# Spectral row groups between the w1 products, and another order inside the norm's backward

## The chip, the cores and the metric

The kernel runs on one core of a Trainium2 chip. The metric is the device time of one execution in microseconds (us). Engines are named as in the profile: PE is TensorE (matmul) and PEld its weight load, DVE is VectorE, ACT is ScalarE, POOL is GpSimd, SP is SyncE. Each engine works through its own queue in order; engines wait for one another through semaphores.

## The reference

The reference is the forward pass of a two-part layer and its gradients. Shapes: x is 2048 x 448 (sequence S by width D), w1 is 2048 x 1792, w2 is 1792 x 2048, the spectral weights are 2048 x 225 (real and imaginary). Inputs and outputs are bf16.

```python
def _A_ref(x, w_r, w_i):
    X = rfft2(x)                       # over sequence and width
    return irfft2(X * (w_r + 1j * w_i))
def _B_ref(x, w1, b1, w2, b2):
    h = _layernorm(x)
    u = gelu(einsum("bsd,sf->bdf", h, w1) + b1)
    return (einsum("bdf,fs->bds", u, w2) + b2).transpose(0, 2, 1)
h  = x + _A_ref(_layernorm(x), w_r, w_i)
h2 = h + _B_ref(_layernorm(h), w1, b1, w2, b2)
```

Outputs are h2 and the gradients of x, w_r, w_i, w1, b1, w2 and b2 for a given grad_out. The change lies in the backward pass: the gradient dh behind the second norm, the spectral transform of dh, and the gradient of x behind the first norm.

## The kernel before

Everything is tiled over 128 partitions. A row index h = 0..15 (NT = 16) stands for the 16 interleaved sets of 128 sequence positions. The two-dimensional transform is done with matmuls against tables, in steps: fft_rows folds four sets h of a group g (three VectorE operations, L303 to L305, into the tile eo) and makes 16 matmuls of 128 x 128 x 128 (L311), four per PSUM tile; each PSUM tile is then copied to zt, on ScalarE ("a", L194) or VectorE ("v", L196) as the string "aava" says. fft_cols then makes the columns, cmul multiplies by the weights, ifft_cols and ifft_rows come back.

The forward pass fills the first 186 us. Behind it lies what the change touches:

1. The w1 loop (L624 to L633). For each h, 14 matmuls (L632) accumulate the product of w1T and du in one PSUM tile pd of 449 columns; column 448 holds the sum that the mean needs. The w1T tiles are loaded by transposing DMAs on SP's queue, through a ring of four.
2. norm_back, called once for each h, turns pd into the row set dh[:, h, :]. It makes the sum of products nm2 (L601, VectorE, with a read-out of the accumulator), the mean's column nm1 (L606, VectorE), the scaled copy v of the whole tile (L608, ScalarE), and two VectorE operations (L611, L612) that put these together. v uses nm1; L611 uses nm2 and v.
3. Behind the loop, fft_rows on dh for groups 0, 1 and 2, then the first block of the w2 gradient, gw2(0) (L653: 16 matmuls and four copies on ScalarE), then fft_rows for group 3, whose matmuls are put behind gw2(0) by hand.
4. fft_cols, cmul, ifft_cols and 16 times ifft_rows. Each ifft_rows ends in a PSUM tile py, on which norm_back is called with mean=False: L601, then v (L610, ScalarE, without a bias), L611, L612, and a store of the gradient of x on POOL's queue.
5. gw2(1) to gw2(13), each 16 matmuls and four copies, three on ScalarE and one on VectorE ("aaav"). In the program they follow the spectral step, but they fill TensorE's time between its matmuls.
6. The w1 gradient (L723, 256 matmuls, all copies on ScalarE), with a second cmul on VectorE for the gradients of w_r and w_i (grad_w) put in after its fourth row set.

The order of the instructions on each engine is not that of the program text alone. A planner at build time walks all instructions by priority, which is their place in the program, and gives an engine that it believes free the first instruction that it believes ready; on the chip the queues then keep that order. `with tc.issue_after(x)` puts what is inside behind x on x's engine. Tiles come from rings: PSUM has three buffers for matmul results (ps_mm: pd and the gradients' blocks) and five for the spectral step (ps_sp); in SBUF, eo comes from a ring of three, v from one of three, junk and the outputs from one of ten. The planner adds the waits for data, for buffers and for PSUM tiles.

Of the kernel before, what the change touches and what calls it, by code (L numbers as in the profile page):

```python
# [13 lines left out]
ALU = mybir.AluOpType  # L14
# [3 lines left out]
P = 128  # L18
S = 2048
D = 448  # L20
DF = 225
F = 1792
NFB = 14
NT = 16
NR = 16
# [88 lines left out]
def kernel(  # L114
# [21 lines left out]
    ve, ac, po, pe = nc.vector, nc.scalar, nc.gpsimd, nc.tensor  # L136
# [7 lines left out]
    def slot(i, shape, name):  # L144
        return big.tile(shape, BF16, tag=f"s{i}", name=name)

    def w4(shape, name):
        return ring.tile(shape, BF16, tag="w4", bufs=4, name=name)

    def e4(shape, name):  # L150
        return ring.tile(shape, BF16, tag="e4", bufs=3, name=name)

    def k1(shape, name, dtype=BF16):
        return ring.tile(shape, dtype, tag="k1", bufs=10, name=name)

    def f2(shape, name):
        return ring.tile(shape, F32, tag="f2", bufs=3, name=name)

    def col(n, name, dtype=F32):
        return ring.tile([P, n], dtype, tag=name, bufs=4, name=name)  # L160

    def ps_mm(shape, dtype=F32):
        return psum.tile(shape, dtype, tag="mm", bufs=3, name="ps_mm")

    def ps_sp(shape, dtype=F32):
        return psum.tile(shape, dtype, tag="sp", bufs=5, name="ps_sp")

    def ld(out, in_, eng=None):
        return (eng or nc.sync).dma_start(out=out, in_=in_)
# [4 lines left out]
    def ld_t(out, in_):  # L174
        return nc.sync.dma_start(out=out, in_=in_, transpose=True)
# [11 lines left out]
    def ld_t4(out, in_):  # L187

        ld_t(out[:, 0:3, :], in_[:, 0:384])
        ld_t(out[:, 3, :], in_[:, 320:448])  # L190

    def ev(out, in_, on):
        if on == "a":
            ac.copy(out=out, in_=in_)  # L194
        else:
            ve.tensor_copy(out=out, in_=in_)  # L196
# [33 lines left out]
    def load_w(dst, on):  # L230
        on(ld, dst[:, 0, :], A_w_r.rearrange("(q r) k -> q (r k)", r=NR))
        on(ld, dst[:, 1, :], A_w_i.rearrange("(q r) k -> q (r k)", r=NR))
# [67 lines left out]
    def fft_rows(src, zt, g, on, behind=None):  # L300
        eo = e4([P, 4, D], "eo")
        a, b = src[:, 4 * g:4 * g + 4, 1:224], src[:, 4 * g:4 * g + 4, 447:224:-1]
        ve.tensor_tensor(out=eo[:, :, 1:224], in0=a, in1=b, op=ALU.add)  # L303
        ve.tensor_tensor(out=eo[:, :, 225:448], in0=a, in1=b, op=ALU.subtract)
        fold = ve.tensor_copy(out=eo[:, :, 0:225:224], in_=src[:, 4 * g:4 * g + 4, 0:225:224])  # L305
        for i in range(4):
            h = 4 * g + i
            pz = ps_sp([P, 4, P])
            with tc.issue_after(behind.ins) if behind is not None else nullcontext():
                for c, o in enumerate((0, 97, 225, 320)):  # L310
                    last = pe.matmul(pz[:, c, :], lhsT=eo[:, i, o:o + P], rhs=kf[:], start=True, stop=True)  # L311
            ev(zt[:, :, :, 8 * h:8 * h + 8], pz[:, :, :].rearrange("p c (s k) -> p c s k", k=8), on[i])
        return last, fold
# [114 lines left out]
    du = slot(7, [P, NFB, 450], "du")  # L428
# [147 lines left out]
    for t0 in range(0, NT, 4):  # L576
# [3 lines left out]
        for j in range(NFB):  # L580
            for i in range(4):
                pe.matmul(p2[i][:], lhsT=w2c[t0 // 4][:, j, i * P:(i + 1) * P], rhs=gT[:, j, :],  # L582
                          start=(j == 0), stop=(j == NFB - 1))
        for i in range(4):
# [3 lines left out]
                                    op0=ALU.add, op1=ALU.add)  # L588
# [3 lines left out]
    for h in range(NT):  # L592
        junk = ring.tile([P, D], BF16, tag="gj", bufs=1, name="junk")
# [2 lines left out]
    ac.copy(out=gb2b[:], in_=gb2[:])  # L596

    def norm_back(ps, mean, xhat, rstd_c, rneg_c, base, out):
        nm2 = col(1, "nm2")
        junk = k1([P, D], "junk")  # L600
        ve.tensor_tensor_reduce(out=junk[:], in0=ps[:, 0:D], in1=xhat, scale=rneg_c, scalar=0.0,  # L601
                                op0=ALU.mult, op1=ALU.add, accum_out=nm2[:])
        v = f2([P, D], "v")
        if mean:
            nm1 = col(1, "nm1")
            ve.tensor_scalar(out=nm1[:], in0=ps[:, D:D + 1], scalar1=rstd_c, scalar2=-1.0 / D,  # L606
                             op0=ALU.mult, op1=ALU.mult)
            ac.activation(out=v[:], in_=ps[:, 0:D], func=ACT.Identity, scale=rstd_c, bias=nm1[:])  # L608
        else:
            ac.activation(out=v[:], in_=ps[:, 0:D], func=ACT.Copy, scale=rstd_c)  # L610
        ve.scalar_tensor_tensor(out=junk[:], in0=xhat, scalar=nm2[:], in1=v[:], op0=ALU.mult, op1=ALU.add)  # L611
        ve.tensor_tensor(out=out, in0=junk[:], in1=base, op=ALU.add)  # L612

    dh = go_r
    w1Tv = B_w1.rearrange("(q h) f -> h q f", h=NT)
    df0 = consts.tile([P, 6 * DF], BF16, tag="df", name="df0")
    di1 = consts.tile([P, 4 * DF], BF16, tag="di", name="di1")
    w_b = slot(6, [P, 2, XW], "w_b")
    for h in range(NT):
        if h == 4:  # L620
            goT = slot(4, [P, 4, S], "goT")
            with tc.issue_after(w1T_last.ins):
                ld_t4(goT[:], grad_out[0])
        if h == 4:  # L624
            with tc.issue_after(w1T_last.ins):
                ld(df0[:], hnd["df0"].ap())
                ld(di1[:], hnd["di1"].ap())
        w1T = w4([P, NFB, P], "w1T")
        w1T_last = ld_t(w1T[:], w1Tv[h])
        pd = ps_mm([P, D + 1])  # L630
        for j in range(NFB):
            pe.matmul(pd[:], lhsT=w1T[:, j, :], rhs=du[:, j, 0:D + 1], start=(j == 0), stop=(j == NFB - 1))  # L632
        norm_back(pd, True, hln[:, h, :], rstd_h[:, h:h + 1], rneg_h[:, h:h + 1], go_r[:, h, :], dh[:, h, :])  # L633


    with tc.issue_after(w1T_last.ins):
        load_w(w_b, lambda load, out, in_: load(out, in_))
    zt2 = slot(2, [P, 4, NR, P], "zt2")
    for g in range(3):
        fft_rows(dh, zt2, g, "aava")  # L640

    g_t = slot(0, [P, 4, F], "g_t")
    ld_t4(g_t[:], gT_d[:])
# [22 lines left out]
    for h in range(NT):  # L666
        if h % 4 == 0:
            xr = e4([P, 4, D], "xr")
            ld(xr[:], xln_d[:, h:h + 4, :], po)
        py = ifft_rows(ab2, di1, h)  # L670
        gx = k1([P, D], "gx")
        norm_back(py, False, xr[:, h % 4, :], rstd_x[:, h:h + 1], rneg_x[:, h:h + 1], dh[:, h, :], gx[:])
        st(rows(out_1[0])[:, h, :], gx[:])
# [43 lines left out]
    for h in range(NT):  # L717
        s4 = w4([P, F], "s4")
        for n in range(4):
            wdt = 512 if n < 3 else 256  # L720
            pw = ps_mm([P, 512])
            for c in range(4):
                pe.matmul(pw[:, 0:wdt], lhsT=hlnT[:, c, h * P:(h + 1) * P],  # L723
                          rhs=du_t[:, c, 512 * n:512 * n + wdt], start=(c == 0), stop=(c == 3))
# [37 lines left out]
```

## Time and profile before

| | |
|---|---|
| median of 3 runs | 382.5 us (381.94 to 383.04) |
| the profiled execution's own time | 377.61 us |
| its span, first to last instruction | 375.8 us |
| granted TensorE clock | 0.999 of full speed |
| PE busy | 350.0 us, 93% of the span |
| DVE, ACT, POOL busy | 235.5, 215.5, 61.3 us |
| w1 products (L632) | 224 matmuls, 186.2 to 229.3 us |
| span from 229.3 to 240.5 us | PE busy 9.02 of 11.20 us |
| span from 283.0 to 317.2 us | PE busy 33.76 of 34.20 us |
| span from 317.2 to 342.0 us | PE busy 23.66 of 24.80 us |

How to read it: the time behind a line is one profiled execution, on the profile's own clock that starts with the first instruction. A row of a timeline has start, duration, engine, line, operation, output, inputs, shapes and count, and in square brackets how long the engine stood idle before it and what ended that. In the lists of waits a row says who waited for whom, the sum, the number of times and the longest. Matmuls are pipelined and their ends are modelled, so that a short hole in TensorE's queue shows smaller as idle time than in the starts of the rows: work it out from the starts.

### The profile page before, as it was taken

The page shows a single profiled execution, that of the slowest core. Times are in us where ns is not written, and L with a number is a line of the kernel's source. Part 1 is how long each engine was busy: PE and PEld are TensorE (multiplying, and loading weights), DVE is VectorE, ACT ScalarE, POOL GpSimd, SP SyncE. Part 2 cuts the span into 40 slices and gives each one's busy share as a digit, 9 for nine tenths or more (in the row PEclk, how much of TensorE's full clock was granted, in tenths as well). Part 3 has the DMA queues.
Part 4 walks back from the last instruction along what each step waited for, and adds up shares of the span by engine and source line. Part 5 has one row for each costly group of instructions (what it writes and reads, how often), then busy time and mean ns, then how long its engine had stood idle before and what let it go on. Part 6 is the DMA issues. An engine that isn't in the chain of part 4 may idle for free.

```text
span 375.8 us, 5768 instructions
## 1 busy us (share of the span) xinstructions
PE 350.0 (93%) x2115; PEld 200.8 (53%) x2115; DVE 235.5 (63%) x557; ACT 215.5 (57%) x415; POOL 61.3 (16%) x107
## 2 busy tenths in 40 slices
PE   0798999989999999999999997999989999999996
PEld 0455666666655555555555555556655555554553
DVE  4863679876745999522267777268995666598000
ACT  3685555345659998740022224967655656676664
POOL 1000000001113111421120000101013422256111
PEclk9999999999999999999999999999999999999999
DMA  7999998999999999891998891932864544956533
GB/s 280 261 291 269 290 253 241 298 324 221 301 251 347 357 333 382 330 285 24 219 204 173 172 254 64 256 83 90 184 181 181 196 162 149 356 211 229 200 153 147
DMA packets 132524, 86.48 MB, mean 230 GB/s; under 512 B 91952, under 2 KB 123824, under 8 KB 131984
## 3 DMA queue, kind: packets, MB, share of 16 engines
q1 hardware_dynamic: 124304, 55.78, 59.9%
q0 software_dynamic: 8048, 30.31, 21.4%
q8 instruction: 16, 0.26, 0.3%
q14 instruction: 12, 0.10, 0.1%
q10 hardware_dynamic: 144, 0.03, 0.0%
HBM read 32.81 MB, written 30.76 MB: 169 GB/s over the span
## 4 chain that ended last, share of the span: by engine, by line
PE 70%; DVE 13%; DMA 7%; ACT 7%; issue 1%; SPq 1%; ACTq 0%; DVEq 0%
PE ps_mm L632 11%; PE ps_mm L653 9%; PE ps_mm L723 8%; PE ps_sp L582 7%; PE ps_mm L434 7%; PE ps_mm L515 6%; PE ps_sp L515 5%; PE ps_mm L582 4%; DMA w2T<-in_B_w_dram 3%; DMA xs_b<-xs_d 2%; DVE t_r L362 2%; DVE t_i L363 2%; DVE gg L349 2%; PE ps_sp L321 2%; PE ps_sp L311 1%; ACT xln L296 1%
## 5 line engine op out<-in xcount | busy, mean ns | idle before, releaser
L194 ACT CAST s<-ps_mm 128x512 bf16<-128x512 f32 (+1 forms) x107 | 57.2, 559 | 19.2 <-PE ps_mm L723 7.5
L653 PE MATMUL ps_mm<-goT,g_t 128*128 128x512 bf16 x224 | 55.3, 379 | 1.5 <-ACT s L194 1.3
L434 PE MATMUL ps_mm<-go_nat,w2T 128*128 128x448 bf16 x224 | 51.2, 361 | 2.1 <-DMA w2T<-in_B_w_dram 2.1
L723 PE MATMUL ps_mm<-du_t,hlnT 128*128 128x512 bf16 (+1 forms) x256 | 49.9, 352 | 0.6 <-ACT s L194 0.5
L608 ACT ACTIVATE v<-ps_mm,nm,rstd_h 128x448 f32<-128x448 f32 x16 | 11.6, 723 | 56.9 <-DVE nm L606 54.9
L632 PE MATMUL ps_mm<-du,w1T 128*128 128x449 bf16 x224 | 43.1, 353 | 0.0
L723 PEld LDWEIGHTS <-hlnT 128*128 128x128 bf16 x256 | 25.0, 98 | 23.1 <-issue 0.9
L582 PE MATMUL ps_sp<-gT,w2c 128*128 128x448 bf16 x140 | 35.6, 352 | 0.0
L172 POOL DMA_DIRECT2D out_dram<-s x29 | 15.6, 539 | 119.0 <-ACT s L194 81.9
L632 PEld LDWEIGHTS <-w1T 128*128 128x128 bf16 x224 | 21.8, 97 | 21.1
L582 PEld LDWEIGHTS <-w2c 128*128 128x128 bf16 x224 | 21.9, 98 | 20.5
L515 PEld LDWEIGHTS <-w1c 128*128 128x128 bf16 x224 | 21.8, 98 | 20.5 <-issue 1.8
L653 PEld LDWEIGHTS <-g_t 128*128 128x128 bf16 x224 | 21.7, 97 | 19.9 <-issue 1.3
L434 PEld LDWEIGHTS <-w2T 128*128 128x128 bf16 x224 | 22.0, 100 | 18.0 <-DMA w2T<-in_B_w_dram 3.3
L349 DVE TENSOR_TENSOR gg<-ps_sp,gi 128x450 bf16<-128x450 f32 x28 | 16.2, 620 | 17.1 <-ACT gi L346 17.1
L582 PE MATMUL ps_mm<-gT,w2c 128*128 128x448 bf16 x84 | 25.0, 352 | 0.0
L515 PE MATMUL ps_mm<-hln,w1c 128*128 128x448 bf16 x112 | 24.3, 352 | 0.7 <-DVE b1col L504 0.5
L194 ACT CAST eo<-ps_sp 128x450 bf16<-128x450 f32 x32 | 17.3, 540 | 12.7 <-PE ps_sp L407 12.4
L311 PE MATMUL ps_sp<-kf,eo 128*128 128x128 bf16 x128 | 9.8, 230 | 15.6 <-DVE mv_x L281 12.1
L515 PE MATMUL ps_sp<-hln,w1c 128*128 128x448 bf16 x112 | 23.1, 352 | 0.0
L587 DVE SCALAR_TENSOR_TENSOR h<-ps_sp,b2col,hr 128x448 bf16<-128x448 f32 x10 | 6.3, 679 | 25.1 <-PE ps_sp L582 25.1
L610 ACT ACTIVATE v<-ps_sp,rstd_x 128x448 f32<-128x448 f32 x16 | 10.1, 634 | 15.7 <-DVE nm L601 15.7
(146 smaller groups left out, 625.7 us busy)
## 6 DMA issues: line engine op xcount, KB each, us to landing
w1c<-in_B_w_dram SPq DMA_DIRECT2D x7, 1024.0 KB, 8.2
w2c<-in_B_w_dram SPq DMA_DIRECT2D x8, 896.0 KB, 11.1
out_dram<-s POOLq DMA_DIRECT2D x14, 512.0 KB, 3.1
out_dram<-s POOLq DMA_DIRECT2D x15, 448.0 KB, 2.8
xs_d<-xs SPq DMA_DIRECT2D x1, 1800.0 KB, 7.7
xs_b<-xs_d SPq DMA_DIRECT2D x1, 1800.0 KB, 8.6
x<-in_A_x_dram SPq DMA_DIRECT2D x4, 448.0 KB, 4.4
go_nat<-in_grad_out_dram SPq DMA_DIRECT2D x2, 896.0 KB, 7.1
```

The source lines that it names most:

```text
L172: return (eng or po).dma_start(out=out, in_=in_)
L194: ac.copy(out=out, in_=in_)
L311: last = pe.matmul(pz[:, c, :], lhsT=eo[:, i, o:o + P], rhs=kf[:], start=True, stop=True)
L349: ve.tensor_tensor(out=gg[:], in0=pr[:], in1=gi[:], op=op)
L434: pe.matmul(pg[:], lhsT=w2T[j][:, t, :], rhs=go_nat[:, t, :], start=(t == 0), stop=(t == NT - 1))
L515: pe.matmul(pu[:], lhsT=wc[:, h, o:o + P], rhs=hln[:, h, :], start=(h == 0), stop=(h == NT - 1))
L582: pe.matmul(p2[i][:], lhsT=w2c[t0 // 4][:, j, i * P:(i + 1) * P], rhs=gT[:, j, :], start=(j == 0), stop=(j == NFB - 1))
L608: ac.activation(out=v[:], in_=ps[:, 0:D], func=ACT.Identity, scale=rstd_c, bias=nm1[:])
L610: ac.activation(out=v[:], in_=ps[:, 0:D], func=ACT.Copy, scale=rstd_c)
L632: pe.matmul(pd[:], lhsT=w1T[:, j, :], rhs=du[:, j, 0:D + 1], start=(j == 0), stop=(j == NFB - 1))
L653: mm = pe.matmul(pw[:], lhsT=g_t[:, c, j * P:(j + 1) * P], rhs=goT[:, c, 512 * n:512 * n + 512], start=(c == 0), stop=(c == 3))
L723: pe.matmul(pw[:, 0:wdt], lhsT=hlnT[:, c, h * P:(h + 1) * P], rhs=du_t[:, c, 512 * n:512 * n + wdt], start=(c == 0), stop=(c == 3))
```

## The change

Two edits.

- In the w1 loop, before the products of h = 10 and of h = 14, fft_rows is called for group 0 and group 1. Its matmuls are put behind the last product issued so far (w1_last). The tile zt2 is allocated ahead of the loop. Behind the loop only group 2 is left (group 3 stays where it was).
- In norm_back, the sum of products (nm2) is made after nm1 and v instead of ahead of them. With mean=False there is no nm1, and there the sum comes after v.

```diff
     def norm_back(ps, mean, xhat, rstd_c, rneg_c, base, out):
-        nm2 = col(1, "nm2")
-        junk = k1([P, D], "junk")
-        ve.tensor_tensor_reduce(out=junk[:], in0=ps[:, 0:D], in1=xhat, scale=rneg_c, scalar=0.0,
-                                op0=ALU.mult, op1=ALU.add, accum_out=nm2[:])
+
         v = f2([P, D], "v")
         if mean:
             nm1 = col(1, "nm1")
...
             ac.activation(out=v[:], in_=ps[:, 0:D], func=ACT.Identity, scale=rstd_c, bias=nm1[:])
         else:
             ac.activation(out=v[:], in_=ps[:, 0:D], func=ACT.Copy, scale=rstd_c)
+        nm2 = col(1, "nm2")
+        junk = k1([P, D], "junk")
+        ve.tensor_tensor_reduce(out=junk[:], in0=ps[:, 0:D], in1=xhat, scale=rneg_c, scalar=0.0,
+                                op0=ALU.mult, op1=ALU.add, accum_out=nm2[:])
         ve.scalar_tensor_tensor(out=junk[:], in0=xhat, scalar=nm2[:], in1=v[:], op0=ALU.mult, op1=ALU.add)
...
+    zt2 = slot(2, [P, 4, NR, P], "zt2")
     for h in range(NT):
+
+        if h in (10, 14):
+            fft_rows(dh, zt2, h // 4 - 2, "aava", w1_last)
...
-            pe.matmul(pd[:], lhsT=w1T[:, j, :], rhs=du[:, j, 0:D + 1], start=(j == 0), stop=(j == NFB - 1))
+            w1_last = pe.matmul(pd[:], lhsT=w1T[:, j, :], rhs=du[:, j, 0:D + 1], start=(j == 0), stop=(j == NFB - 1))
...
-    zt2 = slot(2, [P, 4, NR, P], "zt2")
-    for g in range(3):
-        fft_rows(dh, zt2, g, "aava")
+    fft_rows(dh, zt2, 2, "aava")
```

## The prediction

> **What bounds the kernel now.** I read the page first: the engines' shares and the 40 slices.
>
> ```profile
> PE 350.0 (93%) x2115; PEld 200.8 (53%) x2115; DVE 235.5 (63%) x557; ACT 215.5 (57%) x415; POOL 61.3 (16%) x107
> ```
>
> TensorE is the bound, so I looked only for stretches in which its queue stands still because another engine is late. The chain of work that ended last, listed in order of time, names one right behind the w1 loop (columns: start, duration, what):
>
> ```profile
> 186.37 42.93 PE ps_mm L632 x224
> 229.30 0.68 PE ps_sp L311 x12
> 230.00 0.73 ACT v L608
> 230.76 0.69 DVE junk L611
> 231.78 0.68 DVE junk L601
> 232.70 0.72 ACT v L608
> 233.42 1.94 ACT zt L194 x5
> ...
> 236.82 0.50 ACT s L194
> 237.36 1.02 PE ps_mm L653 x4
> 238.38 0.89 PE ps_sp L311 x16
> ```
>
> The loop itself is solid matmul. Behind it 48 short row matmuls (L311) fill the five PSUM buffers, and their copies queue on ScalarE behind the last two norm rows. The TensorE timeline has two holes there, 0.83 and 1.13 us. Next I took VectorE's timeline for one norm row of the loop:
>
> ```profile
> 203.28 0.68 DVE L601 CUSTOM_DVE_ANT_0 junk<-ps_mm,hln,rneg_h 128x448 bf16<-128x448 f32 x1
> 203.88 0.08 DVE L601 DVE_READ_ACCUMULATOR2_ANT nm<- 128x1 f32 x1
> 203.88 0.21 DVE L606 TENSOR_SCALAR nm<-ps_mm,rstd_h 128x1 f32<-128x1 f32 x1
> 204.97 0.68 DVE L611 SCALAR_TENSOR_TENSOR junk<-hln,nm,v 128x448 bf16<-128x448 bf16 x1 [0.87 <-ACT v L608]
> 205.69 0.39 DVE L612 TENSOR_TENSOR go_r<-junk,go_r 128x448 bf16<-128x448 bf16 x1
> 206.00 0.68 DVE L601 CUSTOM_DVE_ANT_0 junk<-ps_mm,hln,rneg_h 128x448 bf16<-128x448 f32 x1
> ```
>
> A row takes 2.72 us from L601 to L601; TensorE's 14 products take 42.93/16 = 2.68. VectorE is therefore the slower one, and each of the folds (L303 to L305) of groups 0 to 2 pushes it back another 0.67 (0.54 outside the gap, and a shifted start). By the last row it is 2.5 us late (231.78 against products that ended near 229.3). Last I took the second use of the same helper, where the spectral step ends (L610): the waits, then ScalarE's and TensorE's timelines for one row.
>
> ```profile
> ACT v L610 <- DVE nm L601: 15.7, 14, 1.9
> ```
> ```profile
> 291.52 0.63 ACT L610 ACTIVATE v<-ps_sp,rstd_x 128x448 f32<-128x448 f32 x1 [1.02 <-DVE nm L601]
> 292.05 1.06 ACT L194 CAST s<-ps_mm 128x512 bf16<-128x512 f32 x2
> 293.00 0.56 ACT L194 CAST eo<-ps_sp 128x450 bf16<-128x450 f32 x1
> ```
> ```profile
> 290.93 2.54 PE L653 MATMUL ps_mm<-goT,g_t 128*128 128x512 bf16 x11
> 293.61 0.26 PE L411 MATMUL ps_sp<-eo,kinv 128*128 128x225 bf16 x1
> ```
>
> There ScalarE stands idle 1.02 us for a reduction it does not need the value of; its in-order queue then delivers eo late, and TensorE, out of fill matmuls at 290.93 + 11 x 0.215 = 293.3, waits 0.3 us for it.
>
> **The change, part by part.**
>
> *Row groups 0 and 1 moved into the loop.* 32 of the 64 L311 matmuls move. Sixteen take 0.85 to 1.06 us in these rows, so 1.7 to 2.1 us goes into the loop and out of the stretch behind it: nothing on TensorE's sum. Loop end moves from 229.1 to about 230.9. Their eight copies go too: six on ScalarE (0.5 us each; it idles about 2.0 us a row) and two on VectorE (0.60 each, which fit the 0.87 gap). Cover: ScalarE's idle time. Without it, six copies x 0.5 = 3.0 us would delay v rows. No DMA is issued by the step; SP's queue (w1T loads, then w_b) and POOL's keep their order, and zt2's slot has been free since the w2 product read it. The folds already run in the loop at the fourth, eighth and twelfth row and should stay there.
>
> *The mean's column first, in the loop.* The reduction (L601) now stands behind v. Do the two run side by side? In the L610 rows v waits for a reduction that gives it no data; both read the same PSUM tile. I take it that the order holds the other way round as well. Then a row is: column to v 0.34 (203.88 to 204.22), v to the next VectorE step 0.75 (204.22 to 204.97), reduction to its consumer 0.60 + 0.08 + 0.04 = 0.72 (the read-out now stands directly ahead of its user; 0.04 is what L611 to L612 adds), L611 0.72, L612 0.31: 2.84 us, 0.12 more than now, x 16 = 1.9 us on VectorE. The Trainium skill, "PSUM — Partial Sum Buffer", section "PSUM bank collisions raise a hardware error", says that two engines may not touch the same bank and quadrant at once, two reads included, so software has to put them one behind the other. This speaks against the edit; the L610 rows agree, with 14 waits of 15.7 us in all. By that rule the loop row is the 2.84 us above; without it the row would be 2.12 us and the last fold would no longer be late.
>
> *What that does behind the loop.* VectorE's last row ends at 189.09 + 16 x 2.84 + 3 x 0.67 = 236.5 instead of 234.8. Before, a zt copy (0.61) came between it and the last fold; with fewer copies there, the fold follows at once: 236.5 + 1.25 + 0.1 = 237.9 for group 3's matmuls, against 238.2. TensorE's own work would let them start at 230.9 + 0.85 (group 2) + 16 x 0.213 (first gw2 block) = 235.2: VectorE is what is late next. ScalarE was busy without a break from 233.3 to 239.0 and is not any more, so the last zt copies come 0.6 us sooner and the column step begins near 239.9, not 240.53. I take **0.6 us gained**. Ends: TensorE sets the start (235.2, copies included), 2.9 gained; or the three second fold pieces (0.72 each) and three zt copies (0.60) fall outside the gaps, 4.0 later, 3.4 lost. I am nearest to the first value because the present folds show 0.24 us of gap left after two pieces, and a copy is shorter than those. A PSUM buffer of pd is now freed by the reduction's end, 1.77 us into a row: row 12's at about 227.6, wanted for row 15 at 228.1. Covered by 0.5 us only; TensorE would stall for the excess, but VectorE sets the end of that stretch anyway.
>
> *v first, in the second use.* ScalarE's v no longer waits for VectorE: it can start 0.78 us sooner (291.52 less 290.74, L601's start); the reduction waits for v instead, and behind it on VectorE stand L611, L612, the fourth s copy of a gw2 block and later the grad_w products. One hand-over between engines fewer per row. What is TensorE's loss there? From 283.17 to 317.21: 116 gw2 matmuls x 0.215 = 24.9, and 9 rows x 0.78 + 0.39 = 7.4 of short ones: 32.3 of 34.0, idle 1.7. From 317.21 to 339.61: 84 x 0.190 = 15.9 (32.63/172 from the last stretch) and 4.3: 20.2 of 22.4, idle 2.2. Together 3.9 us; 0.78 a row is more than the 0.2 to 0.3 a row lost. Ends: all 3.9 gained, or 5.9 lost (0.66, v and its hand-over, x the nine rows with copies on VectorE). I take 70%, **2.7 us**, because the fill matmuls are placed by a plan that will shift with the new order, and the nearest row (291.52) shows the wait plainly.
>
> **Sum:** 0.6 + 2.7 = 3.3 us. The profiled execution took 377.6 us (span 375.8 and 1.8 around it), so it would be 374.3. The median shown is 382.5, 4.9 above it; less 3.3 it is 379.2.
>
> **The rivals.**
> 1. *Both reads side by side* (no wait between v and the reduction in the loop): group 3 starts at 235.2, 2.3 us more than forecast, 376.9. Against: the L610 waits.
> 2. *The plan eats it*: fewer fill matmuls per row, new holes of the same size; 0.6 stays at most, 382. For: TensorE holes of 0.3 us are small beside a 0.5 us copy.
> 3. *VectorE overruns in the loop*: folds and copies outside the gaps, 4.0 us later than forecast, 383.2.
> 4. *Slower: VectorE's queue in the second use.* The reduction starts 0.66 us later, waiting for v; behind it stands the s copy that gw2 needs for one of its three PSUM buffers. If it comes late by all of that, nine rows cost 5.9 us and the 1.2 of the gain up to 317 is gone: 379.2 + 7.1 = 386.3. It decides from (3.3 - 1.2)/9 = 0.23 us a row. For: VectorE needs 0.60 + 0.72 + 0.72 + 0.31 + 0.60, nearly 3 us, of a 3.5 us row, behind that wait. Against: it idles 0.55 to 1.0 us before L601 now, and the gap for v disappears.
>
> **How the numbers follow.** Forecast 0.50 (own range 377.0 to 381.2), rivals 1 to 4: 0.10, 0.06, 0.08, 0.26. The measured runs spread over 0.3%, 1.1 us, so "same" is 381.4 to 383.6. Faster: forecast and rival 1, 0.60. Same: rival 2 and half of 3, 0.10. Slower: rival 4 and the other half, 0.30. The range runs from 376.2, just past rival 1, to 384.8, the middle of rival 4, leaving out under 2 in 10.
>
> **What the changed profile would show.** In the loop: L311 matmuls in two blocks of 16, rows of 2.84 us on VectorE, reductions released by v; if the rows are near 2.1, rival 1. Behind it: 16 instead of 48 L311 matmuls, group 3 near 237.9. In the second use: no wait of v for L601, reductions waiting for v, and ScalarE's idle 15.7 us gone; TensorE's holes under 1.2 us over the stage. The prediction is wrong if s copies on VectorE hold up TensorE (rival 4), or if the holes stay though v no longer waits.

## The result, and the profile after

| | before | changed |
|---|---|---|
| median (runs) | 382.53 us (6) | 375.85 us (6) |
| ratio, 95% interval | | 0.987 (0.983 to 0.992) |
| profiled execution's time; its span | 377.61; 375.8 us | 375.83; 374.1 us |
| first w1 product starts at | 186.21 us | 189.14 us |
| A: from there to the first column matmul (L329) | 54.32 us | 52.23 us |
| B: from there to the first L411 | 42.25 us | 42.23 us |
| C: from there to the end of the span | 93.02 us | 90.50 us |

The change made the kernel faster, by 1.3% and by 4.8 us if the ratio on record is applied to 382.5; the two medians themselves are 6.7 us apart. The two profiled executions differ by only 1.8 us, because the changed one was 2.9 us later at its first w1 product, where the two programs do not differ yet. So I compare stretches that begin at that product. A is 2.1 us shorter and C 2.5, and B is the same: 4.6 together.

TensorE's timeline of the changed kernel, from the loop to the last row group (start, duration, engine, line, operation, shapes, count, and in brackets the idle time before it):

```profile
189.14 26.99 PE L637 MATMUL ps_mm<-du,w1T 128*128 128x449 bf16 x140
215.97 1.05 PE L311 MATMUL ps_sp<-kf,eo 128*128 128x128 bf16 x16
216.86 10.90 PE L637 MATMUL ps_mm<-du,w1T 128*128 128x449 bf16 x56
227.60 1.05 PE L311 MATMUL ps_sp<-kf,eo 128*128 128x128 bf16 x16
228.49 5.53 PE L637 MATMUL ps_mm<-du,w1T 128*128 128x449 bf16 x28
233.86 1.05 PE L311 MATMUL ps_sp<-kf,eo 128*128 128x128 bf16 x16
234.75 2.98 PE L656 MATMUL ps_mm<-goT,g_t 128*128 128x512 bf16 x12
237.89 1.02 PE L656 MATMUL ps_mm<-goT,g_t 128*128 128x512 bf16 x4 [0.17 <-ACT s L194]
239.12 1.07 PE L311 MATMUL ps_sp<-kf,eo 128*128 128x128 bf16 x16 [0.21 <-DVE eo L305]
```

Two blocks of 16 row matmuls lie between the products and cost 0.9 us each. The holes of 0.83 and 1.13 us behind the loop are gone; those left are 0.17 and 0.21 us. In the kernel before they stood ahead of these row matmuls:

```profile
231.25 0.87 PE L311 MATMUL ps_sp<-kf,eo 128*128 128x128 bf16 x8 [0.83 <-ACT zt L194]
233.25 0.38 PE L311 MATMUL ps_sp<-kf,eo 128*128 128x128 bf16 x4 [1.13 <-DVE zt L196]
```

The last group waits for its fold on VectorE (L305), 49.98 us behind the first product (52.01 before). VectorE's timeline around a fold shows what a row costs now ("..." stands for rows left out; the first and the last row shown are the loop's first and last):

```profile
192.02 0.22 DVE L603 TENSOR_SCALAR nm<-ps_mm,rstd_h 128x1 f32<-128x1 f32 x1 [0.79 <-PE ps_mm L637]
...
211.84 0.21 DVE L603 TENSOR_SCALAR nm<-ps_mm,rstd_h 128x1 f32<-128x1 f32 x1
212.90 0.68 DVE L610 CUSTOM_DVE_ANT_0 junk<-ps_mm,hln,rneg_h 128x448 bf16<-128x448 f32 x1 [0.85 <-ACT v L605]
...
215.32 0.21 DVE L603 TENSOR_SCALAR nm<-ps_mm,rstd_h 128x1 f32<-128x1 f32 x1
215.45 0.62 DVE L304 TENSOR_TENSOR eo<-go_r 128x892 bf16<-128x892 bf16 x1
...
217.71 0.21 DVE L603 TENSOR_SCALAR nm<-ps_mm,rstd_h 128x1 f32<-128x1 f32 x1
217.84 0.38 DVE L613 TENSOR_TENSOR go_r<-junk,go_r 128x448 bf16<-128x448 bf16 x1
...
220.54 0.21 DVE L603 TENSOR_SCALAR nm<-ps_mm,rstd_h 128x1 f32<-128x1 f32 x1
...
237.39 0.39 DVE L613 TENSOR_TENSOR go_r<-junk,go_r 128x448 bf16<-128x448 bf16 x1
```

The reduction (L610) waits for v. From column to column (L603, from 211.84 us on) the rows take 3.48, 2.39 and 2.83 us: the fold pushes one row back, and at the next the plan has put the following column ahead of L613, which brings most of it back.

In the second use the waits have turned round. v no longer appears as a waiter for the reduction; the reduction waits for v:

```profile
DVE junk L610 <- ACT v L607: 16.3, 12, 2.1
```

One row of it, first ScalarE, then TensorE:

```profile
298.52 0.63 ACT L607 ACTIVATE v<-ps_sp,rstd_x 128x448 f32<-128x448 f32 x1 [0.20 <-ACT s L194]
300.38 0.59 ACT L194 CAST s<-ps_mm 128x512 bf16<-128x512 f32 x1 [1.22 <-PE ps_mm L656]
300.86 0.54 ACT L194 CAST eo<-ps_sp 128x450 bf16<-128x450 f32 x1
```
```profile
298.67 2.97 PE L656 MATMUL ps_mm<-goT,g_t 128*128 128x512 bf16 x13
301.47 0.26 PE L411 MATMUL ps_sp<-eo,kinv 128*128 128x225 bf16 x1
```

ScalarE is now idle because it waits for TensorE (1.22 us), not for VectorE, and the short matmuls follow the fills without a hole: 298.67 + 13 x 0.215 = 301.47.

### The profile page after: what moved, and what is told of

It reads as the page before. It is cut to its first block, busy times and chain, and to the rows that moved or that the text cites. A ratio compares the mean times of both kernels' runs of the same rounds, so it can differ in the third digit from the quotient of the medians.

```text
span 374.1 us, 5776 instructions
## 1 busy us (share of the span) xinstructions
PE 350.1 (94%) x2115; PEld 201.4 (54%) x2115; DVE 236.5 (63%) x557; ACT 217.7 (58%) x415; POOL 61.5 (16%) x107
## 4 chain that ended last, share of the span: by engine, by line
PE 67%; DVE 18%; ACT 7%; DMA 4%; issue 2%; SPq 1%; ACTq 0%; DVEq 0%
PE ps_mm L726 12%; PE ps_mm L656 10%; PE ps_mm L434 8%; PE ps_sp L582 7%; PE ps_mm L515 6%; PE ps_sp L515 5%; PE ps_mm L582 4%; DVE junk L610 3%; DVE junk L612 3%; ACT v L605 3%; DMA w2T<-in_B_w_dram 3%; DVE t_r L362 2%; DVE gg L349 2%; DVE t_i L363 2%; PE ps_sp L321 2%
## 5 line engine op out<-in xcount | busy, mean ns | idle before, releaser
L434 PE MATMUL ps_mm<-go_nat,w2T 128*128 128x448 bf16 x224 | 52.3, 367 | 3.7 <-DMA w2T<-in_B_w_dram 3.7
L172 POOL DMA_DIRECT2D out_dram<-s x29 | 15.7, 541 | 113.9 <-ACT s L194 87.8
L311 PE MATMUL ps_sp<-kf,eo 128*128 128x128 bf16 x128 | 9.3, 231 | 13.4 <-DVE eo L305 13.4
L610 DVE CUSTOM_DVE_ANT_0 junk<-ps_sp,xr,rneg_x 128x448 bf16<-128x448 f32 x16 | 10.9, 682 | 16.3 <-ACT v L607 16.3
```

Source lines behind the costliest of these rows:

```text
L172: return (eng or po).dma_start(out=out, in_=in_)
L434: pe.matmul(pg[:], lhsT=w2T[j][:, t, :], rhs=go_nat[:, t, :], start=(t == 0), stop=(t == NT - 1))
```

## Experiments

Stretches A, B and C are read from each run's profile in the same way; "last group" is the start of the last block of L311 matmuls, counted from the first w1 product; "clock" is the granted clock over about 6 us behind the loop, from the middle of the row matmuls on. All ratios are against the kernel before, with 95% intervals.

| run | median us | ratio | last group | A | C | clock |
|---|---|---|---|---|---|---|
| before (profile shown) | 382.5 | | 52.01 | 54.32 | 93.02 | 1.00 |
| before, again | 382.1 (one) | | 53.31 | 55.62 | 93.12 | 0.72 |
| changed | 375.85 | 0.987 (0.983 to 0.992) | 49.98 | 52.23 | 90.50 | 1.00 |
| changed, again | 375.28 | 0.984 (0.978 to 0.990) | 49.98 | 52.23 | 90.50 | 1.00 |
| 1 rows only | 379.42 | 0.990 (0.986 to 0.994) | 49.70 | 51.94 | 92.94 | 1.00 |
| 2 order only | 380.37 | 0.989 (0.985 to 0.993) | 53.40 | 55.71 | 90.51 | 0.76 |
| 3 order in the second use only | 378.6 | 0.990 (0.986 to 0.994) | 52.05 | 54.36 | 90.50 | 1.00 |
| 4 rows, and 3 | 375.62 | 0.983 (0.979 to 0.987) | 49.71 | 51.95 | 90.50 | 1.00 |
| 5 loop's reduction from SBUF | 377.19 (one) | | 49.07 | 51.38 | 90.44 | 1.00 |
| 6 second use's reduction from SBUF | 381.23 | 0.997 (0.992 to 1.002) | 53.05 | 55.36 | 91.45 | 0.76 |
| 7 as 4, rows lapped | 375.1 | 0.983 (0.977 to 0.988) | 49.61 | 51.66 | 90.49 | 1.00 |
| 8 grad_w later | 382.26 | 0.999 (0.996 to 1.003) | 53.26 | 55.57 | 93.30 | 0.72 |
| 9 as 4, grad_w later | 377.1 | 0.986 (0.982 to 0.990) | 49.66 | 51.90 | 90.50 | 1.00 |
| 10 as 7, grad_w later, group 2 on ScalarE | 375.15 | 0.981 (0.977 to 0.986) | 49.33 | 51.57 | 90.51 | 1.00 |

B is 42.18 to 42.26 us in all of them. My theory was that the change is two things that add up: moved rows shorten A, and v ahead of the reduction shortens C. The rivals were that one of the two edits does it all, and that the planner's re-laid fill matmuls, not the waits, make the gain.

**1. Rows only.** norm_back as before, the rest of the change kept.

```diff
     def norm_back(ps, mean, xhat, rstd_c, rneg_c, base, out):
+        nm2 = col(1, "nm2")
+        junk = k1([P, D], "junk")
+        ve.tensor_tensor_reduce(...)
         v = f2([P, D], "v")
...
-        nm2 = col(1, "nm2")
-        junk = k1([P, D], "junk")
-        ve.tensor_tensor_reduce(...)
```

> Row groups moved, norm_back in its old order. Stretch A runs from the first w1 product to the first column matmul of the spectral step behind it (54.3 us before, 52.2 changed), B from there to the first of the short matmuls L411 (42.3 and 42.2), C from there to the end (93.0 and 90.5). Theory 'two parts': moving the rows alone shortens A by taking the copies out of the tail, and leaves C as before: A 52.2 to 52.7, C 93.0, total about 2 us faster than before. Rival 'the order does it all' (v first and the planner's pulling forward of the column): A 53.7 or more, C 93.0, total within 0.6 us of before.

A is 51.94, C 92.94. The moved rows alone make the whole of A's gain: 2.4 us, a little more than expected and a little more than with the new order in the loop.

**2. Order only.** The new norm_back, no rows moved.

> norm_back in its new order, rows not moved. Theory 'two parts': A stays at 54.3 (within 0.5), because a VectorE row costs 2.82 instead of 2.72 us but the next column is taken early three times; C falls to 90.5; total about 2.5 us faster than before. Rival 'the order does it all': A 52.2 as well, total 4.6 us faster. Rival 'the plan decides' (any edit re-lays the fill matmuls and the gains do not belong to either edit): A or C off by more than 1 us from both.

C is 90.51, as the theory says. A, 55.71, is above all that was expected. This execution had a lower granted clock behind the loop, and so had the kernel before in its second profile, with 55.62 (see the section on what was not expected). So most of the excess is not a price of the order. The 0.1 us between these two is no clean price either: where the kernel before has holes of 0.83 and 1.13 us, TensorE has one of 2.88 us here, in which it waits for a zt copy on ScalarE. What the new order in the loop costs without the moved rows at full clock, no run shows.

**3. New order in the second use only.**

```diff
     def norm_back(ps, mean, xhat, rstd_c, rneg_c, base, out):
-        (reduction)
+        if mean:
+            (reduction)
         v = f2([P, D], "v")
...
+        if not mean:
+            (reduction)
```

> New order only where the helper is called without the mean (second use); the loop in its old order, rows not moved. Theory 'two parts': A 54.3, B 42.3, C 90.5, total 2.5 us faster than before. Rival 'the plan decides': C does not repeat 90.5 within 0.7.

54.36, 42.26, 90.50: as expected to within 0.06 us, and the total 1.0% (0.6 to 1.4) faster. The second use is the one place where the new order pays.

**4. Rows, and the new order in the second use only.** norm_back as in 3, the rows moved as in 1.

> Rows moved, new order in the second use only; the mean rows keep the reduction first. If the new order in the loop is worth nothing, as its 0.10 us a row dearer VectorE chain says: A 52.2 to 52.7, C 90.5, total as the changed kernel, 4.6 us faster than before. If the loop's order is a gain in itself, A is 53 or more and the total 1 us or more behind the changed kernel. If the dearer row is a loss, A is 51.2 and the total 1 us ahead.

A is 51.95, so in the loop the new order is a loss of 0.28 us and no gain: between the first and the last of the three values expected. The total cannot be told from the changed kernel's: the intervals 0.979 to 0.987 and 0.983 to 0.992 overlap.

**5. The loop's reduction takes its factor from SBUF.**

```diff
-        ve.tensor_tensor_reduce(out=junk[:], in0=ps[:, 0:D], in1=xhat, ...
+        ve.tensor_tensor_reduce(out=junk[:], in0=base if mean else ps[:, 0:D], in1=xhat, ...
```

> The changed kernel, but the reduction of a loop row multiplies go_r (in SBUF) instead of the products in PSUM, so its sum is another number; everything else is computed as before. Theory 'shared PSUM tile': the reduction waits for v only because both read pd. Then a VectorE row is 2.12 us instead of 2.82, VectorE is no longer late, the last row group starts at 49.0 us behind the first w1 product (TensorE's own work) instead of 49.98, and A is 51.2. Rival 'the wait is something else' (order of the queue, a buffer): the reduction still waits for v, rows 2.82, A 52.2.

The last group starts at 49.07 and A is 51.38: with VectorE no longer late, TensorE's own work sets the end of the loop, as worked out. But the run does not show the row of 2.12 us. The reduction needs nothing from the products any more and ran ahead of the column, and rows took 2.70 us, the last two of them waiting for TensorE's products. So it shows what VectorE's lateness costs (0.9 us), not that the shared tile alone causes the wait in the loop.

**6. The same in the second use, in the kernel before.**

```diff
-        ve.tensor_tensor_reduce(out=junk[:], in0=ps[:, 0:D], in1=xhat, ...
+        ve.tensor_tensor_reduce(out=junk[:], in0=ps[:, 0:D] if mean else base, in1=xhat, ...
```

> The kernel before, but in the second use the reduction multiplies dh (in SBUF) instead of the products in PSUM, so its sum is another number; order of the program as before. Theory 'v's wait made the holes': v no longer waits for VectorE, C falls from 93.0 to 90.5 to 91.0 although nothing was put in another order, total 2 to 2.5 us faster than before. Rival 'the new order let the plan lay the fill matmuls better': C stays above 92.

With the program's order untouched, v's wait for the reduction has gone, and v waits for the matmuls it reads:

```profile
DVE junk L611 <- ACT v L610: 12.3, 16, 1.5
...
ACT v L610 <- PE ps_sp L414: 4.7, 12, 0.6
```

This settles that the wait came from reading the same PSUM tile: v took no value from the reduction in either kernel, and only the tile that the reduction reads was changed. C fell by 1.6 of the 2.5 us, between the two expectations, and the total (0.997, 0.992 to 1.002) cannot be told from the kernel before's. The plan changed as well (7 to 11 fills in a row between 290 and 301 us, where the kernel before has 11 to 13), so this run does not tell how much of the remaining 0.9 us is the plan's.

The traces of the changed kernel and the kernel before settle the rival "the plan". From one L411 to the next the long fill matmuls (gw2 and the w1 gradient) number 13, 13, 11, 12, 12, 13, 11, 12, 12, 13, 13, 17, 15, 17, 16 before and 13, 13, 11, 12, 13, 13, 11, 11, 13, 13, 13, 16, 17, 18, 16 now. The plan hardly moved, and rows with the same fills became shorter: the seventh, with 11, from 3.46 to 3.16 us. So in the changed kernel the gain of C is that of the waits, not of fills laid anew.

**7. Loop rows lapped.** As run 4, with L611 and L612 of a row issued behind the next row's column.

```diff
-            ve.tensor_scalar(out=nm1[:], ...)
+            m = ve.tensor_scalar(out=nm1[:], ...)
+            if prev is not None:
+                with tc.issue_after(m.ins):
+                    prev()               # the last two steps of row h - 1
```

> Rows moved, new order in the second use only (as in the run with A 51.95), and in the loop the last two VectorE steps of a row are put behind the column of the next row, so VectorE does not stand still for v. If VectorE's row time of 2.72 us is what makes it late: rows follow TensorE at 2.68, the last row group starts at 49.0 instead of 49.7 us behind the first w1 product, A 51.2, total 0.7 us ahead of that run (5.4 faster than before). Rival: the last row, which now also waits for the two steps of the row ahead of it, eats the gain: A 51.9 or more.

The rows follow TensorE (reductions at 221.76, 224.44 and 227.13 us: 2.68 apart), but the last row now has its neighbour's two steps and a zt copy ahead of its own: 49.61 instead of 49.71, A 0.3 better. At 51.66 A lies between the two expectations (51.2, and 51.9 or more): what the rival named ate more than half of the gain.

**8. grad_w later**, in the kernel before (`if h == 8` in place of `if h == 3` ahead of grad_w).

> The kernel before, with grad_w's VectorE products put behind the ninth row set of the w1 gradient instead of the fourth, when the second use is over. Theory: of the 2.5 us that C loses, the larger part (1.6) came from the stretch in which v waited behind these products. Then C falls from 93.0 to 91.4, with the old order of norm_back. If the products do not matter (only the reduction's own 0.8 us does), C stays at 93.0 within 0.3. The tail behind the w1 loop is as before: last row group at 52.0 us behind the first w1 product and A 54.3 where the granted clock stays at 1.00 there, 53.3 and 55.6 where it falls to about 0.75.

The edit did not do what I wanted. The planner put the products where they had been: VectorE's order is that of the kernel before, instruction for instruction, and v waited 15.9 us for reductions (15.7 before). It is a third profile of the kernel before, with C at 93.30, and says nothing on the products. That they delay v is therefore read from the trace only (below), not tried.

**9 and 10.** Run 4 with grad_w later, and run 7 with grad_w later and "aaaa" for group 2.

```diff
-        if h == 3:
+        if h == 8:
             grad_w()
...
-    fft_rows(dh, zt2, 2, "aava")
+    fft_rows(dh, zt2, 2, "aaaa")
```

> Rows moved, new order in the second use only, and grad_w's products behind the ninth row set. If v no longer waits for VectorE in the second use anyway, moving the products gains nothing more: A 51.95, C 90.5 (90.2 at best), total as without it. If TensorE's holes of that stretch still come from VectorE, C 89.5. The clock behind the loop stays at 1.00.

> The same, with the last two VectorE steps of a loop row behind the next row's column (A 51.66 in the run with it), and group 2's copy on VectorE given to ScalarE, so that 0.60 us less stands ahead of the last fold. If VectorE's last row sets the start of group 3: last row group at 49.0 instead of 49.6, A 51.1 to 51.3, C as in the run beside it. Rival: ScalarE, with four copies of group 2 and four of the first gw2 block, is late instead: A 51.6 or more.

Run 9 repeats run 4 in its stretches, as it must, since grad_w did not move: VectorE's order is that of run 4, instruction for instruction. Run 10's last group starts at 49.33, 0.3 above TensorE's own 49.0, and A is 51.57, just under the rival's 51.6; but it is VectorE's last fold that the group waits for (it ends at 239.40, the group starts at 239.47 us), not ScalarE. Runs 7 and 10 are 0.6 to 0.7 us ahead of the changed kernel by the sum of their stretches (184.35 and 184.26 against 184.96); their times (375.1, 375.15 against 375.28 and 375.85) do not separate them from it.

## Why the prediction was right, and where it was not

*Forecast 379.2, measured 375.85; the ratio puts it at 377.7.* The median as it stands is just below 376.2, the low end of the range; by the ratio the time lies inside it. The direction and the two mechanisms were right: 1, 3 and 4 show that they add (A 51.95 with the rows, C 90.50 with the order, B untouched). The size of one term was wrong, and one effect was missing.

*Rows moved: 0.6 us forecast, 2.1 measured.* TensorE's side was right: the blocks cost 0.9 us each in the loop, the copies fit, the products run without a hole, and the last group waits for VectorE. The step that failed is VectorE's sum, "189.09 + 16 x 2.84 + 3 x 0.67 = 236.5", 47.4 us from the first row to the last. Measured: 192.02 to 237.78, 45.8. The row itself was nearly right (2.82, and 2.76 in the first three, against 2.84), but a fold with the row behind it costs 3.48 + 2.39 - 2 x 2.82 = 0.23 us, not 0.67, because the planner pulled the next column ahead of L613. I had taken the fold's price from the trace of the old order and left it unchanged for the new one. With the old order in the loop (run 4) the fold keeps its price and the row is 2.72: 45.5 us (192.08 to 237.55), the same within 0.3, so the edit inside the loop is worth nothing. The 0.3 us that sooner zt copies were to add between group 3 and the column step came to 0.06 (2.31 us before, 2.25 now).

*The rule on PSUM.* The loop rows of 2.82 us, with 14 waits of the reduction for v (9.0 us), are the value by the row and the rule of the Trainium skill, "PSUM — Partial Sum Buffer", section "PSUM bank collisions raise a hardware error", not the 2.12 of reads side by side. Rival 1 fell.

*v first in the second use: 2.7 us forecast, 2.5 measured.* From the first L411 to the tenth after it TensorE gained 0.8 us (35.72 with 122 fills against 35.15 with 123, at 0.215 a fill), from there to the last L411 1.5 us (20.72 with 78 against 19.57 with 80, at 0.190), and 0.2 behind it. Counted as the forecast counted (0.78 for the short matmuls of a row), TensorE's holes between the first and the last L411 went from 3.7 to 1.4 us; the forecast had said under 1.2. That the 70% came so near is partly luck: the first of the two stretches gave back about half of its idle time, the second three quarters. The larger part lies where v stood behind grad_w's products on VectorE. In the kernel before, ScalarE waited 1.92 us there:

```profile
328.69 0.63 ACT L610 ACTIVATE v<-ps_sp,rstd_x 128x448 f32<-128x448 f32 x1 [1.92 <-DVE nm L601]
```

*Rival 4*, the slower one, did not come about: the reduction waits for v, 16.3 us in all, and the copies behind it on VectorE still came in time, since C fell to 90.5 wherever the order was new. *Rival 2* (the plan eats it) fell with C, as the fills above show too. *Rival 3* fell with A.

*What was missing* is the granted clock in the hole behind the loop, next section. It adds to the gain in those executions of the kernel before that have it, and would make the gain in time (4.8 us by the ratio here, 6.2 in the repeat) larger than the 4.6 us of the two profiles at full clock. The intervals of both ratios hold 4.6 us too, so the times alone do not show it.

## What to carry to other kernels

When two engines read one PSUM tile, the program's order decides which queue stands still for the other; let the engine that feeds TensorE read first, and the one with slack wait. Price a small piece of work on a queue from the new order, not the old one: the planner fills gaps anew, and a piece that was outside a gap can come to lie in one. And when an edit re-times something that a planner places, look at the order first: run 8 shows an edit that changed the program and not the queue.

## What had not been expected

**A hole halves the clock, in some executions.** The page of the kernel before shows full clock throughout, and so I priced the holes at their length. I also expected the three stretches to repeat within 0.1 us. Profiled again, the same kernel ran the work behind the holes at half clock, and A was 1.3 us longer. A row has the stretch, its length, the busy time of PE, PEld, DVE, ACT and POOL and, third from the end, the granted clock, in stretches of 2 us behind the loop; first the kernel before, again:

```profile
234.00:236.00 2.00, 0.77 (x8) 0.52 (x8) 1.97 (x6) 0.99 (x3) 0.00 (x0) 1.00 0.00 0
236.00:238.00 2.00, 1.59 (x16) 1.37 (x17) 1.88 (x4) 2.00 (x5) 0.00 (x0) 0.81 0.00 0
238.00:240.00 2.00, 2.00 (x12) 1.17 (x10) 1.62 (x3) 2.00 (x5) 0.00 (x0) 0.50 0.48 95
240.00:242.00 2.00, 2.00 (x10) 0.77 (x8) 0.23 (x2) 1.03 (x3) 0.00 (x0) 0.84 1.28 289
```

and the changed kernel, the same part in one stretch:

```profile
234.70:241.00 6.30, 5.87 (x41) 2.78 (x39) 4.82 (x12) 5.67 (x11) 0.54 (x1) 1.00 0.39 84
```

The clock falls after TensorE has been busy 0.77 of 2 us, and stays at half for 3.41 us; A is then 55.4 to 55.7 us instead of 54.3, 1.1 to 1.4 us more. All six profiles with the rows behind the loop have holes there, the two of 0.83 and 1.13 us (within 0.03), or in run 2 the one of 2.88. Four had the low clock (before again, runs 2, 6 and 8) and two had not (before, run 3). All eight with the rows moved kept the full clock. So moving the rows also takes away a cost that one profile of the kernel before did not show. The Trainium skill, "TensorE: Matmul & The Clock Gate", section "Part 1: The HAM clock gate (the "warmup" mystery)", says that the clock goes to half after an idle window of about 3.4 us, and that the window runs freely. The clock of 0.50, the 3.41 us and its coming in some executions only agree with that. But here holes of 0.83 and 1.13 us with eight short matmuls between them were enough, so the holes need not be as long as the window.

That the phase of such a window matters can be read from the traces. In the second profile of the kernel before, the granted clock changes at 87.05, 90.47, 237.24 and 240.65 us: 3.41, 43 x 3.413 and 3.41 us apart. In every trace the changes lie on such a grid, whose place differs from execution to execution. The two steps of the grid that hold the holes in the kernel before (full clock), and the one step that holds most of them in its second profile (half clock from its end on):

```profile
228.49:231.90 3.41, 2.47 (x32) 1.87 (x30) 2.47 (x8) 1.69 (x3) 0.00 (x0) 1.00 0.00 0
231.90:235.32 3.42, 2.29 (x28) 1.64 (x26) 3.35 (x8) 2.62 (x6) 0.00 (x0) 1.00 0.00 0
```
```profile
233.82:237.24 3.42, 1.60 (x17) 1.13 (x18) 3.35 (x8) 2.41 (x6) 0.00 (x0) 1.00 0.00 0
```

In the four executions with the low clock one step has TensorE busy for 1.23 to 1.76 us, and the clock is halved for the whole of the next; in the two others the holes fall across two steps of 2.14 to 2.53 us each. No threshold follows: in run 6 a step with 1.41 us, from 84.68 us on, left the clock full.

**The time ahead of the loop varies by 5 us.** The first w1 product started at 186.2 to 191.3 us over these runs, in programs that are the same up to there. In the stretch from 85 to 96 us the granted clock was 1.00 in the five executions that got there earliest (186.2 to 188.2) and 0.69 to 0.84 in the nine others (189.1 to 191.3). TensorE also waits for loads of w2T ahead of the loop, 2.1 us in all in the profile shown and up to 5.6 (run 2); why they come later in some executions is open. The execution whose profile stands first here was shorter (377.6 us) than any other of that kernel in the comparison runs (378.2 to 385.4). One profile of one execution is a poor base for a total; stretches that start at a common instruction agree within 0.1 us wherever the clock is full.
